# First batch: the halves of the squared norms enter through TensorE's accumulation

## The chip, the cores and the metric

One Trainium2 chip, one core of it. The metric is the time of one execution on the device in microseconds (us), the median of a few runs. Lower is better.

## The reference, cut to what matters

The reference is a linear attention with exponential random features, followed by two feed-forward layers over its output. The change is in the features of q and k, for the first of four batches:

```python
# q, k, v: (4 batches, 8 heads, 576 tokens, 64); omega: (128, 64)
q_s, k_s = q * 64**-0.25, k * 64**-0.25
def phi(x):
    proj = x @ omega.T                       # 128 features
    sq = np.sum(x * x, axis=-1, keepdims=True) / 2
    h = proj - sq
    h = h - np.max(h, axis=-1, keepdims=True)
    return np.exp(h) / np.sqrt(128)
...
num / den                                    # q' (k'^T v), q' sum(k')
# then x = (tokens, 512): g = h * sigmoid(1.702 h), h = x @ w_in (512 x 2048); x = g @ w_out
# then x = (x @ w_a * x @ w_b) @ w_out2, inner width 1536
```

Subtracting sq shifts all 128 features of a token alike, so the maximum over h, subtracted next, shifts with it.

## The kernel before, in words

The 576 tokens of a head are split into 512 (per batch eight heads make four pairs of heads, hp 0 to 3, with eight tiles of 128 tokens a pair) and a rest of 64 that is collected over the heads. The batches run one after the other; batch 0 has a way of its own. Its q and k stay in f32: for each pair of heads (named k0_0 to k0_3 and q0_0 to q0_3; the rests are k0_r and q0_r) `features` makes four transposes on TensorE into one bank of PSUM (L718), an eviction to SBUF that scales by 32 (L665 on ScalarE, L664 on VectorE for the names in `EVX`), and eight projections, f32 matmuls of 64 x 128 by 64 x 128 (L729): two heads, j 0 and 1, lie in the lower and the upper 64 rows of the array. The trace records each f32 matmul as two passes.

Beside that, ScalarE squares the raw tile in place (L762) and VectorE sums the squares (L764). When the projections are done, VectorE takes the maximum over the features, two reductions of 512 elements (L812), then two small operations form the bias of the exponential, first maximum minus sum (mh), then its negative minus sum (nb, L818). ScalarE runs eight exponentials with that bias (L778). For k, f32 matmuls with v accumulate the sums over tokens (L873, rest L871). For q, the features are transposed (L897), evicted (L899), multiplied with these sums (L904), divided by the denominator on VectorE (L929 to L934), and transposed (L959) into xT, the f16 high and low parts that the first feed-forward layer reads (L960, L961). The rests run through `rest_phase`, which has the same steps at half or quarter size (L673 to L706).

The weights arrive as raw words and are converted in chunks: four passes of 1024 elements per chunk on VectorE (L492, L532, L540, L499) and one on ScalarE (L550), for 16 chunks of the first layer and more later. The first layer's products (L992 to L994, L1027 to L1029) are dense f16 matmuls that begin when batch 0 is through; features of batches 1 to 3 (f16, L745, L746) are mixed in between. `fillers` issues matmuls whose result nobody reads (L1465, 15 in two calls of 5 and 10; ten more at the start, L1516).

The program is written out by generators that are stepped in turns, but the order on each engine's queue is not theirs: `ORDER` holds, for TensorE, ScalarE, VectorE and SyncE, one permutation of all instructions, and the last lines of the kernel tie each instruction to the one before it. An engine works through its queue strictly in that order. SyncE (SP) issues nearly all loads, so a load that waits for a buffer holds up those behind it.

Of the kernel before, what the change touches and what calls it, by code (L numbers as in the profile page):

```python
# [10 lines left out]
F32 = mybir.dt.float32  # L11
# [3 lines left out]
ALU = mybir.AluOpType  # L15
# [30 lines left out]
    "vKUb9t6x70/dp2+U5L228gZIhie6e74HO2/4pD23G/u9vd6DXQ62m7qz4HafDrb3cf90gyvDvxH3KW9g5o2X9O/BjZcs37tb3POR"
    "9yzkPQt5r/i6h6ke3tH9l+Puue6e6+657p7r7rnCvz/+8fHlvjT/zgiG9uXu4L7Vuu+ywl/v/ryje3Tr4Z+Suz//sHi/N4Dr7qDs"
    "wBG/95x8+nL/+vKa75/GSfFv3X3NN67y5a93V+MfxfuDlx/c77187+7+nsZyGu8ZrKd/zu5xdgZv2KYAudGUN5pSNN3rLe/1lm8P"
    "tqv7Su/rK6/v7UDc77kg7oVYDk750/338B7TdrbeHuKf7fuC7oPbcbmnp+7pKf/67k/vc9wH942IvhHR94i3nfqX976tvm+r7w7a"
    "v97+Od5/j+8/4vet9tOD7w+efnCf11u4128dv0OI8Xtw7qVR9+qpe/XUcULv4+5VUTfG68Z4+bXkBnrdQK8brHWDtcMvEPfJb+T0"  # L50
    "jZy+sdE3Njo85D55+uKdC5X7J7/P3ACusoP7tjyv30Ru/FV5H/cHNzb65YA5ko7L/ZNfQ9qh89O7KwfW7zU3/vqe5H770319NxL7"
    "nvO+J7SdmbdfZvw2c3+dubsaR+hGYt1IrPHX+9JuEJZfj+5dpe5dpe7rq/v66gZm3cCsG5h1A7ME5svjXnfPeb/c35HuYZ972Ofe"
    "Geb46T04NzrrLTbuTm901n0LJTpdTPfVz32DcwNunIp7kvv46/11rD3EL3N3zzeQ5gbN3PCZe5jmHqa5oTI3VOaGytwjPi97ubu/"
    "b2vu25qXv/rl7h7EG0h9/ODu4L7Bvu+t73vr4yH3EB8/uIf4hlSn3zjv425I9Q2pviHVQio97r6Pt98o76u6l8HcuH/eAOnyxbVw"
    "d3XjpW+8tHgpF87d1T15z3tInvdFPu/l93RZ+eUzffHr5f3BfS3P+1qe9xp8Pvzp/mJ6Y+15j+nzvt/nfftPb/9GxPO+86d3fmOj"
    "b2z0+Kkn8oP7ju7x63v8+uUhgvo+7u6g7eDlcfflvjzlfVXHq7rPcQ/O8x6c5z04z3sMnuUF3b/eUHn6nfketecNlefbr8x+x747"
    "uK/ldXfwsgO/n4uNe82Mg9O+56f31+z7HK/wO/z9bfu+wdd9g6/7Bl/3yV/3BLzuCXjd+Jt76OYeurnHeR52f0/ePQsjMI9f3u9m"
    "94le+0R3p2WnPj3cV3rP+as85O7q3lrm3lom/PXu+d5a5t435obF3BM694TOPaFzT+ikTzR3i3v8xtt3IMaf7u59SLl31pfPGmLD"
    "+3WF3mP1uqH8cpn6xOMjj888PvTc4zL70ec+m5frU9N9jhmfoe4W9znm6Xq7B6x9ue/cJXkP9txjOiXu707vcRkfysoZvOfoPtHT"
    "CbiX1eteVq/jOezqHr97Jb/al/tTH5k85X3NLxfx0w7uX4+36rXcx92bwuveFF4+ZfmY5bOZD183dl83bN/3Fvm+p/vlee/+xs3t"  # L60
    "huPccJwbjuMivuE4NxznhuO4c719rrxb3Pvu8+Favcfeh7n75XkP+/Me9ud9q8/jqrgPvjH5DJ8O7+PuXep5A+QZXtr9WOj6vaHy"
    "vKHyvKHyDKf7HqH7vK/7vO/7vO+Hz6j3A+IN0bfjci/J98MXn15ddPfZyqfR+2z3zDydmRuxzxuxT3epeySf7RPu3aJdW3eLe6af"
    "7Ynuu3SJ3wB53gB5+rwrCH3i9ZHXZ+T9kHyf456K59M94m7xcgNwH7pv+jg9zvl9q/csvO5ZeN2z8Lpn4XXPwuuehdfbgbhv8B7n"
    "9/Gq/PW+33uc3/c4v+9xfpdP0ven912+72F/O9gOrF2Fu8Dd/f3BK3zvBuF9yMuxT3ep+z7eNvN5/r7Ie+Jf95y/7sl7iat7Bl/O"
    "zD0Lr3sWXg9Xo1fls//96b3sX4kD7rb3sn/dy/6Vfnpf831V73tm3vcEvNsO7g/ug9/7kPvT+/re90J83x287w7e95bxvneBdzkQ"
    "952Pze5fkzzc11K+eCLPcX96z/77nv33PfvvwRB3p/f28L63h/c9++979t/3nL9vCLxvCLzFHzjBITcY3k97vju4V/f7Xt3ve0d6"
    "3zvS+17d7/H67Ap43Mf5BP6gAw888OADj1otwSV44cEXHoDhUbsVKnHEbti9b9i9b9i9X17lfaZ7V3i7K7iGbti9b9i9b9i9b9i9"
    "KQyG4TDC7u0JCMzj4QUt36zfLLastuCWR6zaeKEPLzT2q0eilsdZ1LFPNvFwgD/g44fw4sFtHuDmEWtF+9UuUceDmDzA0AMKPfjQ"
    "Aws9CNFjYejsk3sWvvMAPI/nfrWH5wKVP+f+2d7ozgP+PKjOg+g84M6DjzxQyQOTPDjJA5Q8XitSHo92Hr2PtC0peRCRxzoZJFsJ"
# [1549 lines left out]
```

## Time and profile before

| what | value |
|---|---|
| median of 3 runs | 864.57 us (863.15 to 868.79) |
| profiled execution | 867.92 us, span 866.1 us |
| TensorE (PE) busy | 854.5 us, 99% |
| VectorE (DVE) busy | 677.8 us, 78% |
| ScalarE (ACT) busy | 457.6 us, 53% |
| granted TensorE clock, mean | 0.999 |

The span is from the first to the last instruction of the profiled execution; the time beside it is that execution's own. "Busy" is the share of the span in which an instruction ran. Matmuls are pipelined and their ends are modelled, so the start of one matmul and the start of the next tell more of the pace than a duration does. PEld is the weight load, which runs beside the matmuls.

### The profile page before, as it was taken

How to read it: one execution, taken by the hardware profiler on the slowest of the kernel's cores; microseconds unless marked ns; L12 is line 12 of the kernel's file. 1: busy time of each engine (PE TensorE's matmuls, PEld its weight loads, DVE VectorE, ACT ScalarE, POOL GpSimd, SP SyncE). 2: the span in 40 equal slices, each digit the busy share in tenths (PEclk: the TensorE clock that was granted, in tenths of full speed). 3: DMA queues.
4: the chain of work that ended last, by engine and by line, in shares of the span. 5: the costliest groups of instructions: out<-in, count | busy, mean ns of one | idle time of the engine just before them, and what ended most of it. 6: DMA issues, size and time to landing. Idle time of an engine off the chain costs nothing.

```text
span 866.1 us, 17321 instructions
## 1 busy us (share of the span) xinstructions
PE 854.5 (99%) x7064; PEld 618.5 (71%) x7064; DVE 677.8 (78%) x1224; ACT 457.6 (53%) x1087; POOL 1.5 (0%) x11
## 2 busy tenths in 40 slices
PE   9999999999999999999999999999999999999997
PEld 7865555455554555444468888889888899888896
DVE  4999999999989987799111489968999658456766
ACT  5988786698668766654233554444543313123221
POOL 0000000000000000000000000000000000000000
PEclk9999999999999999999999999999999999999999
DMA  9766799866745344865110125322422203123312
GB/s 272 209 180 172 180 238 234 213 135 146 198 96 134 77 104 81 149 202 211 50 49 2 57 103 183 138 65 86 164 105 86 42 8 100 76 103 122 86 44 73
DMA packets 138735, 107.71 MB, mean 124 GB/s; under 512 B 107168, under 2 KB 120480, under 8 KB 136608
## 3 DMA queue, kind: packets, MB, share of 16 engines
q1 hardware_dynamic: 138080, 106.05, 44.9%
q8 instruction: 55, 0.90, 0.4%
q10 hardware_dynamic: 576, 0.56, 0.2%
q14 instruction: 24, 0.20, 0.1%
HBM read 71.07 MB, written 17.69 MB: 102 GB/s over the span
## 4 chain that ended last, share of the span: by engine, by line
PE 86%; DVE 8%; DMA 3%; ACT 2%; issue 1%; ACTq 0%; DVEq 0%
PE y L1027 6%; PE y L1028 6%; PE y L1029 6%; PE ph L994 6%; PE ph L993 6%; PE ph L992 6%; PE paA L1151 3%; PE paA L1153 3%; PE paA L1152 3%; PE pbA L1151 3%; PE pbA L1153 3%; PE pbA L1152 3%; PE oA L1247 3%; PE oA L1249 3%; PE oA L1248 3%; PE pa L729 1%
## 5 line engine op out<-in xcount | busy, mean ns | idle before, releaser
L1028 PE MATMUL y<-gl,w_out 128*128 128x512 f16 (+1 forms) x320 | 113.4, 358 | 0.4 <-DVE gl L1014 0.4
L1029 PE MATMUL y<-gh,w_out 128*128 128x512 f16 (+1 forms) x320 | 113.4, 358 | 0.0
L1027 PE MATMUL y<-gh,w_out 128*128 128x512 f16 (+1 forms) x320 | 109.5, 358 | 0.3 <-ACT gh L1013 0.3
L1014 DVE SCALAR_TENSOR_TENSOR gl<-th,gh 128x512 f16<-128x512 f32 (+1 forms) x80 | 50.4, 635 | 65.8 <-ACT gh L1013 65.4
L993 PE MATMUL ph<-xT,w_in 128*128 128x512 f16 x256 | 96.8, 379 | 0.0
L992 PE MATMUL ph<-xT,w_in 128*128 128x512 f16 x256 | 96.0, 379 | 0.2
L994 PE MATMUL ph<-xT,w_in 128*128 128x512 f16 x256 | 96.0, 379 | 0.0
L1151 PE MATMUL pbA<-forms,w_b 128*128 128x256 f16 (+1 forms) x240 | 61.1, 262 | 0.0
L1152 PE MATMUL pbA<-forms,w_b 128*128 128x256 f16 (+1 forms) x240 | 61.1, 262 | 0.0
L1153 PE MATMUL pbA<-forms,w_b 128*128 128x256 f16 (+1 forms) x240 | 61.0, 262 | 0.0
L1152 PE MATMUL paA<-forms,w_a 128*128 128x256 f16 (+1 forms) x240 | 61.0, 262 | 0.0
L1153 PE MATMUL paA<-forms,w_a 128*128 128x256 f16 (+1 forms) x240 | 61.0, 262 | 0.0
L1151 PE MATMUL paA<-forms,w_a 128*128 128x256 f16 (+1 forms) x240 | 61.0, 262 | 0.0
L1247 PE MATMUL oA<-w_o,ab 128*128 128x256 f16 x216 | 58.9, 273 | 0.3 <-DVE o L1255 0.3
L1249 PE MATMUL oA<-w_o,ab 128*128 128x256 f16 x216 | 58.9, 273 | 0.0
L1248 PE MATMUL oA<-w_o,ab 128*128 128x256 f16 x216 | 58.9, 273 | 0.0
L1161 ACT COPY ka<-paA 128x512 f32<-128x512 f32 (+1 forms) x30 | 16.3, 544 | 77.6 <-PE paA L1153 77.6
L1013 ACT ACTIVATE gh<-th 128x512 f16<-128x512 f32 (+1 forms) x80 | 47.0, 589 | 16.9 <-DVE th L1004 6.6
L1029 PEld LDWEIGHTS <-w_out 128*128 128x128 f16 x320 | 31.3, 98 | 29.0 <-issue 0.9
L993 PEld LDWEIGHTS <-w_in 128*128 128x128 f16 x320 | 31.3, 98 | 28.6 <-issue 1.4
L1161 ACT COPY kb<-pbA 128x512 f32<-128x512 f32 (+1 forms) x30 | 16.3, 542 | 66.4 <-PE pbA L1153 63.9
L994 PEld LDWEIGHTS <-w_in 128*128 128x128 f16 x320 | 31.3, 98 | 28.0 <-DVE w_in L499 0.4
(232 smaller groups left out, 2391.2 us busy)
## 6 DMA issues: line engine op xcount, KB each, us to landing
wraw<-in_moe_w_out_dram SPq DMA_DIRECT2D x14, 1024.0 KB, 6.3
forms<-fd SPq DMA_DIRECT2D x8, 1792.0 KB, 7.5
wraw<-in_moe_w_in_dram SPq DMA_DIRECT2D x8, 1024.0 KB, 5.7
fd<-forms SPq DMA_DIRECT2D x4, 1792.0 KB
wraw<-in_moe_w_a_dram SPq DMA_DIRECT2D x6, 1024.0 KB, 6.0
wraw<-in_moe_w_b_dram SPq DMA_DIRECT2D x6, 1024.0 KB, 7.5
vt<-in_v_dram SPq DMA_DIRECT2D x16, 256.0 KB, 5.5
rawq<-in_q_dram SPq DMA_DIRECT2D x16, 256.0 KB, 4.6
```

Of the source, the lines that this page charges most:

```text
L992: nc.tensor.matmul(ph[:, :n], w[:, 0, c, fs], xh(c), start=(c == 0), stop=False)
L993: nc.tensor.matmul(ph[:, :n], w[:, 0, c, fs], xl(c), start=False, stop=False)
L994: nc.tensor.matmul(ph[:, :n], w[:, 1, c, fs], xh(c), start=False, stop=(c == KC - 1))
L1027: nc.tensor.matmul(o, w[:, 0, f % 4, cs], gh[f][:, :n], start=(f == 0), stop=False)
L1028: nc.tensor.matmul(o, w[:, 0, f % 4, cs], gl[f][:, :n], start=False, stop=False)
L1029: nc.tensor.matmul(o, w[:, 1, f % 4, cs], gh[f][:, :n], start=False, stop=(f == FC1 - 1))
L1151: nc.tensor.matmul(o[:, i], wh, xh, start=first, stop=False, skip_group_check=True)
L1152: nc.tensor.matmul(o[:, i], wh, xl, start=False, stop=False, skip_group_check=True)
L1153: own["pe"] = nc.tensor.matmul(o[:, i], wl, xh, start=False, stop=final, skip_group_check=True).ins
L1247: nc.tensor.matmul(bank[:, t], lh, wh, start=first, stop=False, skip_group_check=True)
L1248: nc.tensor.matmul(bank[:, t], lh, wl, start=False, stop=False, skip_group_check=True)
L1249: nc.tensor.matmul(bank[:, t], ll, wh, start=False, stop=final, skip_group_check=True)
```

## The change

The sums of squares of batch 0 are no longer made by VectorE. ScalarE squares the transposed tile, read from PSUM, into the raw tile's place, and a second projection with a constant matrix `negs` (every element -1/PROJ = -256, PROJ being the scale that the exponential undoes) adds the negative sum of squares to every feature of the token in the same accumulation. The maximum is then taken over the finished difference, and one small operation makes the bias of it. `EVX` puts six evictions on VectorE instead of two. The memset that made a zero tile for the ten first matmuls now makes `negs`, and those matmuls read it. Batches 1 to 3 keep their way.

`ORDER` is planned anew for all four engines. TensorE has 6952 instructions instead of 6880, VectorE 1208 instead of 1224, ScalarE 1013 instead of 1017, SyncE 225 as before. Decoded, the first batch's part of it reads as follows. On TensorE the 72 projections of before stand in 14 unbroken blocks; 27 times two neighbours lie in opposite halves of the array, and 18 stand alone. The 144 of after stand in 9 blocks, 53 such neighbours and 38 alone, among these the last eight of k0_3 and all sixteen of q0_2. Fillers: before, 12 between the projections of k0_1 and the transposes of k0_3 and three before the sums of k0_1; after, five ahead of the fourth transpose of k0_0, one behind the transposes of k0_1, four between the transposes of k0_2 and k0_3, five ahead of the projections of q0_3. After the last projections of k0_3 come the transposes of q0_2, q0_1 and q0_3, then the projections of q0_r and q0_0, then the transposes of q0_r's features (L705), the sums of k0_3, and the projections of q0_1 and q0_2. On ScalarE the eight exponentials of k0_3 are followed by the eviction and the square of q0_1 and then q0_r's exponentials. On VectorE three steps of other work stand ahead of k0_3's second maximum, and three more ahead of q0_r's maxima.

```diff
 ORDER = (
-    "eNp93b2OK1mzINZXaVy7De74IylPgMYfQICcwRiCrHEkZyBH0Lur9gqyuvu7d2R09TlVzCSZGZmnuCJ2xP/zb//5P/3b//THf3n8"
...
 )
...
@@ -385,7 +387,7 @@
     CW, RB, FB = 256, 2, 2
     RW = CW // P
     START_W, LAG, POST_W, AL, EARLY = 0, 2, 8, 2, 3
-    VT, FILL, EVX = 4, 10, ('q0_1', 'q0_r')
+    VT, FILL, EVX = 4, 10, ('k0_1', 'k0_2', 'k0_r', 'q0_0', 'q0_3', 'q0_r')
     RAW = {"k": 3, "q": 4}
     SQACC = "1"
     EVD = ()
@@ -674,22 +676,23 @@
                 pt[:, u * P : (u + 1) * P], x[:, 2 * u : 2 * u + 2, :].rearrange("p n d -> p (n d)"), own["ident"]
             )
         scaled(f"{kind}0_r", xt.rearrange("p u m -> p (u m)"), pt[:, 0 : 2 * P])
-        sq, mx, mh, nb = (
-            pool.tile([P, NHP], F32, tag=f"rest{t}", name=f"{t}_rest{kind}", bufs=1) for t in ("sq", "mx", "mh", "nb")
+        mx, nb = (
+            pool.tile([P, NHP], F32, tag=f"rest{t}", name=f"{t}_rest{kind}", bufs=1) for t in ("mx", "nb")
         )
-        nc.scalar.activation(out=x, in_=x, func=AF.Square, scale=SQROOT)
+        x2 = x.rearrange("p n d -> p (n d)")
+        nc.scalar.activation(out=x2, in_=pt[:, 0 : 2 * P], func=AF.Square, scale=SQROOT)
+        x2 = x2.rearrange("p (u m) -> p u m", m=P)
         yield
-        nc.vector.tensor_reduce(out=sq, in_=x, axis=AX.X, op=ALU.add)
         pvs = [psp()[:, 0 : 2 * M].rearrange("p (u m) -> p u m", m=M) for _ in range(2)]
         for u in range(2):
             for j in range(2):
                 c = slice(j * D, (j + 1) * D)
-                nc.tensor.matmul(pvs[j][:, u, :], xt[c, u, :], om_f[c], start=True, stop=True)
+                nc.tensor.matmul(pvs[j][:, u, :], xt[c, u, :], om_f[c], start=True, stop=False)
+                nc.tensor.matmul(pvs[j][:, u, :], x2[c, u, :], own["negs"][c], start=False, stop=True)
         yield
         for j in range(2):
             nc.vector.tensor_reduce(out=mx[:, j::2], in_=pvs[j], axis=AX.X, op=ALU.max)
-        for o, i0, scale in ((mh, mx, PROJ), (nb, mh, -1.0)):
-            nc.vector.scalar_tensor_tensor(out=o, in0=i0, scalar=scale, in1=sq, op0=ALU.mult, op1=ALU.subtract)
+        nc.vector.tensor_scalar(out=nb, in0=mx, scalar1=-PROJ, scalar2=None, op0=ALU.mult)
         e = pool.tile([P, NHP, M], F32, tag="e", name=f"e_rest{kind}", bufs=2)
         for hp in range(NHP):
             nc.scalar.activation(
@@ -720,13 +723,17 @@
                     own["ident"],
                 )
             own["xt", nm] = scaled(nm, xt.rearrange("p u m -> p (u m)"), pt)
+            x2 = x.rearrange("p t d -> p (t d)")
+            nc.scalar.activation(out=x2, in_=pt, func=AF.Square, scale=SQROOT)
+            x2 = x2.rearrange("p (u m) -> p u m", m=P)
 
             def project():
 
                 for u in range(NT):
                     for j in range(2):
                         c = slice(j * D, (j + 1) * D)
-                        nc.tensor.matmul(pvs[j][:, u, :], xt[c, u, :], om_f[c], start=True, stop=True)
+                        nc.tensor.matmul(pvs[j][:, u, :], xt[c, u, :], om_f[c], start=True, stop=False)
+                        nc.tensor.matmul(pvs[j][:, u, :], x2[c, u, :], own["negs"][c], start=False, stop=True)
 
         else:
             x16 = pool.tile([P, T, 2, D], F16, tag="A", name=f"x16_{nm}")
@@ -746,8 +753,8 @@
                     nc.tensor.matmul(pv[:, u, :], xt[:, i, :], om_l, start=False, stop=True)
 
         groups, pairs = (GROUPS_F, PAIRS_F) if nm[1] == "0" else (GROUPS, PAIRS)
-        sq = pool.tile([P, T], F32, tag="sq", name=f"sq_{nm}")
-        TB = x.shape[1]
+        if nm[1] != "0":
+            sq = pool.tile([P, T], F32, tag="sq", name=f"sq_{nm}")
 
         def squares(lo, hi):
             for t in range(lo, hi):
@@ -759,9 +766,11 @@
             yield
             squares(0, NT)
         else:
-            nc.scalar.activation(out=x, in_=x, func=AF.Square, scale=SQROOT)
-            yield
-            nc.vector.tensor_reduce(out=sq[:, 0:TB], in_=x, axis=AX.X, op=ALU.add)
+            if nm[1] != "0":
+                nc.scalar.activation(out=x, in_=x, func=AF.Square, scale=SQROOT)
+            yield
+            if nm[1] != "0":
+                nc.vector.tensor_reduce(out=sq, in_=x, axis=AX.X, op=ALU.add)
         extra()
         yield
         if nm[1] in SQACC:
@@ -813,8 +822,11 @@
                     out=mx[:, ms], in_=pv[:, : len(g), :], axis=AX.X, op=ALU.max
                 )
                 if gi - 1 == pair[-1]:
-
-                    for o, i0, scale in ((mh, mx, PROJ), (nb, mh, -1.0)):
+                    if nm[1] == "0":
+                        nc.vector.tensor_scalar(
+                            out=nb[:, : z - a], in0=mx[:, : z - a], scalar1=-PROJ, scalar2=None, op0=ALU.mult
+                        )
+                    for o, i0, scale in ((mh, mx, PROJ), (nb, mh, -1.0)) if nm[1] != "0" else ():
                         own["nb"] = nc.vector.scalar_tensor_tensor(
                             out=o[:, : z - a], in0=i0[:, : z - a], scalar=scale, in1=sq[:, a:z],
                             op0=ALU.mult, op1=ALU.subtract,
@@ -1510,10 +1522,11 @@
         nc.scalar.dma_start(out=own["om"], in_=omega)
         a_load(att, "k", 0, 0)
         a_load(att, "k", 0, 1, nc.scalar)
-        zero = att.tile([P, 2, P], F16, tag="zero", name="zero", bufs=1)
-        nc.vector.memset(zero, 0.0)
+        own["negs"] = att.tile([P, M], F32, tag="negs", name="negs", bufs=1)
+        nc.vector.memset(own["negs"], -1.0 / PROJ)
+        zero = own["negs"].bitcast(F16).rearrange("p (a b) -> p a b", a=2)
         for _ in range(10):
-            nc.tensor.matmul(idle[:, 0:256], zero[:, 0], zero.rearrange("p a b -> p (a b)"), start=True, stop=True)
+            nc.tensor.matmul(idle[:, 0:256], zero[:, 0], own["negs"].bitcast(F16), start=True, stop=True)
         warm = att.tile([P, 1], F32, tag="warm", name="warm", bufs=1)
         nc.vector.memset(warm, 0.0)
         nc.scalar.activation(out=warm, in_=warm, func=AF.Exp)
```

## Rows read from the trace of the kernel before

**Rows 1.** The chain of work that ended last, shares of the span by engine.

```profile
PE 86%; DVE 8%; DMA 3%; ACT 2%; issue 1%; ACTq 0%; DVEq 0%
```

**Rows 2.** Stretches: us, then busy us (count) of PE, PEld, DVE, ACT, POOL; clock, DMA, GB/s.

```profile
5.00:17.40 12.40, 12.12 (x64) 9.46 (x65) 5.51 (x13) 7.04 (x20) 0.00 (x0) 1.00 1.10 277
17.40:60.00 42.60, 40.25 (x356) 34.55 (x354) 38.89 (x88) 38.08 (x132) 0.00 (x0) 1.00 0.73 201
60.00:360.00 300.00, 297.23 (x2195) 159.18 (x2195) 276.88 (x585) 217.69 (x605) 0.00 (x0) 1.00 0.66 154
```

**Rows 3.** Timeline of TensorE, 48 to 59 us: start, us, instructions, idle before.

```profile
47.99 0.38 PE L959 MATMUL pa<-ident,xf_q 128*128 128x128 f32 x2
48.82 1.11 PE L904 MATMUL pa<-kv,eT_q 128*128 128x65 f32 x8 [0.46 <-ACT eT_q L899]
...
57.50 0.50 PE L959 MATMUL pa<-ident,xf_q 128*128 128x128 f32 x3
58.78 0.22 PE L745 MATMUL pa<-om_h,xt_k 128*128 128x128 f16 x1 [0.78 <-DVE xf_q L934]
```

**Rows 4.** Groups on VectorE, 5 to 62 us: count, busy us, mean ns, idle before.

```profile
L540 DVE SCALAR_TENSOR_TENSOR wf<-wraw,wf 128x1024 int32<-128x1024 int32 x4 | 4.9, 1219 | 0.0
...
L764 DVE TENSOR_REDUCE sq_q<-rawq 128x8 f32<-128x512 f32 x4 | 2.7, 683 | 0.0
...
L664 DVE TENSOR_SCALAR xt_q<-pa 128x512 f32<-128x512 f32 x1 | 0.7, 682 | 0.0
L818 DVE SCALAR_TENSOR_TENSOR nb_q<-mh_q,sq_q 128x8 f32<-128x8 f32 x4 | 0.7, 164 | 0.0
...
L664 DVE TENSOR_SCALAR xt_restq<-pa 128x256 f32<-128x256 f32 x1 | 0.4, 417 | 0.0
L682 DVE TENSOR_REDUCE sq_restk<-restk 128x4 f32<-128x256 f32 x1 | 0.4, 409 | 0.0
```

**Rows 5.** Groups on ScalarE, 5 to 62 us.

```profile
L778 ACT ACTIVATE e_q<-pa,nb_q 128x128 f32<-128x128 f32 x32 | 8.9, 394 | 0.0
...
L762 ACT ACTIVATE rawq<-rawq 128x512 f32<-128x512 f32 x4 | 2.6, 651 | 0.2
...
L665 ACT ACTIVATE xt_k<-pa 128x512 f32<-128x512 f32 x4 | 2.4, 604 | 2.7 <-PE pa L729 2.3 <-PE pa L718 0.4
```

**Rows 6.** Timeline of TensorE, blocks of projections (L729) and what follows them.

```profile
23.33 1.16 PE L729 MATMUL pa<-om_f,xt_k 64*128 64x128 f32 x8
24.42 0.66 PE L718 MATMUL pa<-ident,rawq 128*128 128x128 f32 x4
...
28.71 0.66 PE L718 MATMUL pa<-ident,rawq 128*128 128x128 f32 x4
29.29 1.16 PE L729 MATMUL pa<-om_f,xt_q 64*128 64x128 f32 x16
30.38 1.11 PE L873 MATMUL pa<-vt,e_k 128*128 128x65 f32 x8
...
36.55 0.71 PE L729 MATMUL pa<-om_f,xt_q 64*128 64x128 f32 x8
37.20 0.98 PE L897 MATMUL pa<-ident,e_q 128*128 128x128 f32 x7
```

**Rows 7.** Timeline of TensorE, the fillers (L1465) and what follows.

```profile
13.15 2.74 PE L1465 MATMUL idle<-om_h 128*128 128x256 f16 x12
15.69 1.06 PE L718 MATMUL pa<-ident,rawk 128*128 128x128 f32 x4
16.68 1.58 PE L729 MATMUL pa<-om_f,xt_k 64*128 64x128 f32 x16
...
22.06 0.50 PE L1465 MATMUL idle<-om_h 128*128 128x256 f16 x3
22.40 0.39 PE L871 MATMUL pa<-vm,e_restk 128*128 128x130 f32 x2
```

**Rows 8.** Waits of SP's queue, 0 to 62 us: us in total, times, longest.

```profile
SPq L625 <- DVE sq_q L764: 7.4, 3, 3.7
```

More of the change, by code (lines that the diff above doesn't have):

```diff
@@ new lines @@
+    "p37+v+6+P8/XP8/VP9u0k/NE98j3lPKew/Nnm+fPNs+fbZ4/27x+/tc/W/S9FD/POT+Pv37+PT/bvO7z/fzu/fPv+TnU+2efudfr"
+    "Xryfc3jfK/jz+PPnv5/33z/7Pe9z/Dz2use5x/jZ5/Xz+Ote3HtFX/dq38v6/tnifS/vve7ve43vxX/fAbhX+X1HIQzDfey+lLeB"
+    "uiP1uL9/3PF53CM87haPO0SP+zSPe4zH3f9x9whHuv+6F/SU57xHMcj3Qp97hc+9jOdex3Mv9LlX+bTtnNzdZKeGg95D3Rlw7vU9"
+    "9/qee13PvbDnXtlzL825c+CkmXT3Tadxf2fC3BcTD/+6E8qLubPlpH/dI6fZ5z/vGdw5ctrv7nbtP+/h76Q5d/ac8cDddzxwn3I8"
+    "YJJ74B7vDu258+fcQT13RM8dynPnyHm6G7ys++gd03MH9dxRPXdYz507506aY3Rf7h03iu3ubm8b332N8J1B522Tu++dQMdAG/Y7"
@@ new lines @@
+    "vnEvdtyLHfdih5vO3XYvdri97sWOO+ZxxzzumMfD7+4eD0dxn94Le+dc3PkWd57FnWPhLt7b+B7lzq24syTuLAm3rXs23eV3X7fu"
+    "HYC4gxJ3FOIOaNwpFXdKxZ1IUTa5R7mDHHeQ0y1/D5r3oOnOd9A74aIcxR73oHcso71x3E3uIMcdy7hjHm2T+xx3uGNsd/e9Yx53"
+    "aOOOedzxjfF2dDe+gxxjj7vxHd+4kzXuZI07WeNO1rijH0/vYHePO/BxBz7uwMfL29jd4w583PGNO7RxhzvuSMcd37hDG2/vdfd4"
+    "d5DjzpK4cyNe/vMe/u3HPcod+Lz3Qt57Ie+9kPdeyId3UW+h99E7oHkHNI9H7zvbHfi8A5934PNOnzz2uI/e4c47kfJ44737emv0"
+    "/nyvZN6rm/fC5r2m2d6M77Pd65f3+uW9sHkvYt6LmPci5r2IeS9i3quWT++y93dhzO8T+QNxZ056x/cWf2dO7hv/PcqdJWmW3ImU"
@@ new lines @@
+    "dyLlnUh5J1LeCZJ3WmT58+ElOLW7xx3pvCOdd7Tyjlbe0co7WnnHKO/FzpfX5kzvHk973Oe4A5ovf4j8Z98/N/dvzz218lftnlo5"
+    "tTuMeQeq7vDUHa0yWncY8w5j3SGre9nrjlvda1938Op49D5wHOA+cK9V3WtV91rVvVblj6k/Wndy5Z1ceSdXvj2R0/D38p7unVz1"
+    "cOR70OOP8D3enSB1nIvTuNvd94267xvlD6q/rvcSl7+d5QF/de+h9m/q/c870nVHuu5I171+da9f3etXd+Dr6Y/v3eMOQIUf/ljf"
+    "H/fs6559vf3hvvvesy9nf69p3etXrt+9uv3wR/x1f9z/vJepwx/1+1f9XqZ2me4bSt03lEofE+6R0wOG8R75zrW686Xu6Ned/NU+"
+    "T9zt7uSvO/mrbXef8l77vteqfYbxYnzyuDdE3VlXPoDcWVf3/qh7f9TY457unTR9J03fSdMu9tPV8MD94OXTzL3s7TPLvex9L3v7"
@@ L302 @@
[L302 to L306 removed]
+    "24e3D28f3j68fXj78Pbh7cPbh7cPbx/ePrx9ePvw9uHtw9uHtw9vH94+vH14+/D24e3D24e3D28f3j68fXj78Pbh7cPbh7cPbx/e"
@@ L307 @@
+    "h5HeqIcPj59M233Pjw157MrQjQzsB40/YYz3N46wtp+/tv/8aPvOim/owCz4Tbjdm2zfO56/lP8L+H+c3g1Yv0GCP8mt+96R3wxX"
+    "t5xx69+wgrcL7xDeGv5kAu/7wjcf+SP28dX+P1m57jxvE+6+jXHEl/LrT9Ti/Eei30jGbyqtW9y4/C2V9vk/zsrdu9ZIuXP/pMi6"
+    "Gd1zbv7n+Wca7jeB9u8ZuP2bgfv6zbv9jX1sZu3rG+IwiIZt6f38JtU+fxH+N1l2Yb5/xf5PQu77m2P7J0X2b2mz/R9N/t/l2P49"
+    "Wfa//r//H7miBh4="
 )
```

519 lines of the change are left out of this document (251 added, 268 removed).

## The prediction

> **What bounds the kernel now.** I read the chain of work that ended last first. It puts 86% of the span on TensorE and 8% on VectorE [rows 1]. The stretches say where the 8% can be: TensorE is busy 297.23 of 300.00 us from 60 to 360 us, but 40.25 of 42.60 us between 17.4 and 60 us, where VectorE is busy 38.89 us and ScalarE 38.08 us [rows 2]. The change lives in that stretch and the 12.4 us before it. So the question is which engine ends that stretch, and the reader should look for TensorE standing still in it.
>
> The order of TensorE's instructions shows that it seldom does. Ends of matmuls are modelled, so I go by starts. Two transposes (0.11 us each) start at 47.99 and the next group at 48.82 us: 0.61 us lost, of which the view calls 0.46 idle. Three start at 57.50, the next at 58.78 us: 0.95 lost, 0.78 called idle [rows 3]. So true losses are about 1.26 times the idle shown, and the 2.35 us of the stretch [rows 2] become an estimated 3.0 us. From 60 to 360 us there are another 2.8 us at most. VectorE and ScalarE are nearly full beside TensorE, but TensorE is the one that hardly waits. **Whatever is added to TensorE must find its room in 3.0 + 2.8 us.**
>
> **What leaves VectorE and ScalarE.** VectorE loses eight sums of squares at 0.68 us and two of the rest at 0.41 (6.3 us), and of 20 small operations at 0.16 us ten remain, in another form that I price alike (1.6 us). It gains evictions: four of 0.68 and two of 0.42 in place of one of each, +2.5 us [rows 4]. Net -5.4 us, all of it work that stands beside TensorE's. ScalarE loses three whole evictions and a half one, some 2.2 us at 0.60 each [rows 5]. Its squares stay the same in number and read PSUM instead of SBUF; the eviction, which reads PSUM already, takes 0.60 against the square's 0.65 us, so I price this at nothing (ends -0.05 and +0.05 each). The merged memset and the filler's other operand cost nothing: same sizes, same engine. These savings shorten the end only through waits of TensorE that they remove.
>
> **What enters TensorE.** A further 72 projections, each recorded as two f32 passes. The price stands in their blocks of before. A block of 16 records on both halves of the array takes 1.09 us from its start to the next (29.29 to 30.38); 8 records on one half alone also take 1.09 us (23.33 to 24.42); 8 records on both halves take 0.65 us (36.55 to 37.20) [rows 6]. So a projection costs 0.22 us, a neighbour on the other half rides along free, and a block has 0.21 us of its own, plus 0.14 us before it: four transposes in front take 0.58 us, not 4 x 0.11. That is 0.35 us a block.
>
> Read from the two orders: before, 27 pairs and 18 alone in 14 blocks; after, 53 pairs and 38 alone in 9 blocks. That is 91 - 45 = 46 more times 0.22 us: +10.1 us; five blocks fewer: -1.8 us. Fillers: 12 ran at 0.212 us, 1.2 GHz, and three at 0.113 us, 2.4 GHz [rows 7] (the granted clock column reads 1.00 before 17.4 us too, but the early fillers show the half rate). After, ten come early and five late: -0.2 us. **TensorE: +8.1 us.** I take the full-rate price, though many added projections run at the half rate: TensorE is busy 12.12 of 12.40 us before 17.4 us [rows 2], so what is put there pushes other work past the rise.
>
> **What it can absorb.** Of the 3.0 us I take 2.0, since the gaps at 48 and 58 us sit in the normalisation of the last heads, which the change leaves as it is. Of the 2.8 us after 60 us I take half, 1.4, as VectorE, 5.4 us lighter, is further ahead with the weights.
>
> **What waits newly.** (a) The square is now between a head's transposes and its second projections: 0.65 us. Other heads' matmuls stand ahead of it in the order; if they run out it is 0.65 us at the first head. I take 0. No row of before has VectorE and ScalarE reading one bank of PSUM together, as six tiles now could, with eviction and square on different engines; even in sequence they take no longer than now, when ScalarE does both (0.68 + 0.65 against 0.60 + 0.65 us), so I keep 0, with 0.08 a tile as the upper end.
>
> The Trainium skill ("PSUM — Partial Sum Buffer", PSUM bank collisions raise a hardware error) says that two engines must not use one bank in the same partitions at once and that the compiler back end keeps them apart. By that the six pairs would run one after the other, each about 0.6 us later than side by side, an estimate of +3.4 us if TensorE waited for every one: 873.8 us against the median.
>
> (b) Five fillers stand ahead of the first head's fourth transpose, 1.06 us; the next transposes need a load in any case; 0, at most 1.06. (c) The raw tiles come free after the second projections, not after VectorE's sums. Already now the loads of raw tiles stand 7.4 us in SP's queue behind those sums [rows 8], with weight loads queued behind them. TensorE uses those tiles many us later, so I take 0, ends 0 and about 2 us for one late weight chunk (a conversion step is 1.22 us [rows 4]). (d) The transposes of the remainder of q. After the last eight projections of head k0_3 TensorE has 12 transposes, 12 pairs and two blocks: 1.3 + 2.6 + 0.7 = 4.7 us. In that time the other two must do a maximum and the bias (0.85 us), eight exponentials (2.2), an eviction (0.60), a square (0.65) and four exponentials (1.6) [rows 4, 5]: 5.9 us. So TensorE waits 1.2 us there. The path by VectorE has three more steps ahead of the remainder's maximum: 0.85 + 3 x 1.22 + 1.0 + 1.6 = 7.1 us, a wait of 2.4. I take 1.2. Queued behind it are head k0_3's own sums, two blocks of projections and all of the q phase.
>
> **Sum**: 8.1 - 2.0 - 1.4 + 1.2 = +5.9 us. The profiled execution took 867.92 us (span 866.1), so 873.8, or 0.68% more; against the median of the runs, 864.57 us, that is **870.4 us**.
>
> **Rivals.** 1, slower by more than 1%: the wait at the remainder's transposes is large. VectorE has three conversion steps ahead of k0_3's second maximum too; if they start late, up to 3.7 us come on top of the 2.4, and the old waits aren't recovered: 5.9 + 4.9 + 2.0 = +12.8, 877.4 us. It decides from a wait of about 4 us on. For it: VectorE is busy 91% of that stretch. Against: TensorE, being later itself, gives VectorE time to catch up. Chance 0.17.
>
> 2, no loss: the rate rises earlier. Now it rises inside the block that starts at 16.68 us, near 17.3, behind 12 dense fillers from 13.15 us, and not in the f32 work ahead of them [rows 7]. The new order has one long block of 32 projections right behind the first transposes, from 7 or 8 us by the prices above, 20 x 2 x 0.212 = 8.5 us long at half rate. If the rate rose in the middle of it, at about 11.6 us, 5.7 us at half rate would shrink by 2.9. With all 5.8 us of waits absorbed and no new one: 8.1 - 5.8 - 2.9 = -0.6, 864 us. The Trainium skill ("TensorE: Matmul & The Clock Gate", Part 1: The HAM clock gate) says that sustained activity releases the throttle; that speaks for this rival, but the trace's f32 work did not release it. Chance 0.14.
>
> 3, faster: VectorE ends the stretch, and the 5.4 us come off: 862.5, or 859.2 us against the median. For it: VectorE's 91%. Against: TensorE, at 94%, has no room for 8.1 us more. Chance 0.05.
>
> **How the numbers follow.** The forecast, TensorE's added work partly absorbed, +2 to +8.6 us, has 0.64. One per cent, about what a measurement can tell from no change, is 8.6 us. Faster by that needs more than rival 3 gives: 0.02. Slower: rival 1 and the forecast's upper edge, 0.22. Within: 0.76. The range 865 to 877 us leaves out rival 3, half of rival 2 and the upper part of rival 1, together about 0.2.
>
> **What would show it.** Right: the projections of the pairs of heads have 256 records in place of 128, in blocks at the prices above; the first dense products of the first feed-forward layer start some 5 us later; from there both traces run parallel. VectorE's stretch has idle time, or more conversion steps done by the same point. Wrong: TensorE idle for over 4 us at the remainder's transposes (rival 1); fillers or projections at the full-rate price before 15 us (rival 2); or TensorE's dense part starting no later than now (rival 3). A replanned order that costs or gives more than 3 us after 100 us would be outside all of these.

## The result, and the profile after

The changed kernel took 874.25 us (median of 4 runs, 873.12 to 875.91), the kernel before beside it 863.97 us: a ratio of 1.0106, 95% interval 1.0078 to 1.0134. In a later set of runs (e10 below) it was 870.92 against 865.50 us, 1.0068 (1.0043 to 1.0093). So it is slower, by 5.4 us in one set and 10.3 in the other. The forecast, 5.9 us more (870.4 us), lies near the lower of the two; why the sets differ is a part of what follows. The profiled execution took 874.63 us (span 872.8).

In the chain of work that ended last, VectorE's share halved, to 4% from the 8% of [rows 1]:

```profile
PE 88%; DMA 4%; DVE 4%; ACT 3%; issue 1%; SPq 0%; ACTq 0%; DVEq 0%
```

The same stretches as in [rows 2], same columns:

```profile
5.00:17.40 12.40, 11.47 (x128) 9.90 (x127) 5.27 (x12) 6.76 (x19) 0.00 (x0) 1.00 1.12 273
17.40:60.00 42.60, 41.26 (x410) 38.61 (x410) 40.28 (x75) 37.84 (x131) 0.00 (x0) 1.00 0.85 229
60.00:360.00 300.00, 296.52 (x2209) 159.31 (x2209) 271.84 (x584) 215.18 (x600) 0.00 (x0) 1.00 0.68 150
...
```

TensorE has 128 instead of 64 records before 17.4 us and 410 instead of 356 up to 60 us, and is idle 1.34 instead of 2.35 us in that second stretch. Its waits from 5 to 60 us (us in total, times, longest):

```profile
PE pa L916 <- ACT eT_q L911: 1.0, 2, 0.7
PE pa L675 <- DMA restk<-in_k_dram: 0.9, 1, 0.9
PE pa L735 <- ACT e_k L787: 0.2, 1, 0.2
```

Not one is for a square or a second projection. At the remainder's transposes (L708), where rival 1 had its wait, TensorE's timeline goes on without a gap:

```profile
33.35 0.27 PE L735 MATMUL pa<-om_f,xt_q 64*128 64x128 f32 x1
33.47 0.38 PE L736 MATMUL pa<-negs,rawq 64*128 64x128 f32 x2
33.78 0.55 PE L708 MATMUL pa<-ident,e_restq 128*128 128x128 f32 x3
```

Where eviction and square of one PSUM tile are on two engines, the square begins when the eviction has ended. VectorE's row, then ScalarE's:

```profile
22.00 0.69 DVE L666 TENSOR_SCALAR xt_q<-pa 128x512 f32<-128x512 f32 x1 [0.19 <-PE pa L721]
```

```profile
22.73 0.60 ACT L727 ACTIVATE rawq<-pa 128x512 f32<-128x512 f32 x1 [0.42 <-DVE xt_q L666]
```

All six such tiles show this, 0.03 to 0.05 us behind the eviction's end. From PSUM a square of 512 elements takes 0.59 to 0.66 us here (0.65 from SBUF, [rows 5]).

TensorE reached its upper clock at 5.0 us in this execution, at 17.4 in the profiled one of before. That is the first entry of each profile's record of the granted clock; the clock column of the stretches shows 1.00 ahead of it too, but the pace there is the lower one [rows 7]. Here the clock rose inside the five fillers: they ran in 0.70 us, start to next start, and the transposes behind them at 0.11 us each:

```profile
4.71 0.86 PE L1477 MATMUL idle<-om_h 128*128 128x256 f16 x5
5.41 0.71 PE L721 MATMUL pa<-ident,rawk 128*128 128x128 f32 x5
```

So the two profiles don't show the price of the change side by side: the one of before lost some 3 us to a late rise (2.7 at its end, by e5 below). And at 376 us the changed kernel has a stretch that before lacks (TensorE's timeline):

```profile
376.84 0.38 PE L1006 MATMUL ph<-xT,w_in 128*128 128x512 f16 x1
378.56 1.02 PE L1039 MATMUL y<-gh,w_out 128*128 128x512 f16 x4 [1.34 <-ACT gh L1025]
380.13 0.38 PE L1040 MATMUL y<-gl,w_out 128*128 128x512 f16 x1 [0.55 <-DVE gl L1026]
380.35 0.47 PE L1041 MATMUL y<-gh,w_out 128*128 128x512 f16 x1
380.61 0.63 PE L1040 MATMUL y<-gl,w_out 128*128 128x512 f16 x1
381.04 0.63 PE L1041 MATMUL y<-gh,w_out 128*128 128x512 f16 x1
```

The starts of the last two stand 0.43 us apart, twice the 0.215 us of the rows of 378 us: the granted clock of 380.5 to 384 us is 0.51, the lower level of 1.2 GHz (columns as in [rows 2]):

```profile
380.50:384.00 3.50, 3.50 (x11) 1.24 (x9) 3.50 (x7) 1.48 (x2) 0.00 (x0) 0.51 0.67 257
384.00:390.00 6.00, 6.00 (x29) 2.72 (x28) 4.34 (x6) 2.01 (x4) 0.00 (x0) 1.00 0.01 3
```

ScalarE's timeline says why gh is late. The conversion of w_a, which stands ahead of the Silu in its new order, waits for a sum of VectorE:

```profile
376.30 1.06 ACT L552 ACTIVATE w_a<-sx 128x1024 f16<-128x1024 f32 x1 [2.21 <-DVE sx L528]
377.26 0.58 ACT L1021 ACTIVATE th<-ph 128x512 f32<-128x512 f32 x1
377.87 0.63 ACT L1025 ACTIVATE gh<-th 128x512 f16<-128x512 f32 x1
```

A ruler for all the kernels: the rest of the program is the same in each, so I counted TensorE's work back from the end, every matmul at its full-rate time (0.213 us for 512 columns, 0.107 for 256 or for an f32 pass of 128 rows, 0.053 for a pass of 64 rows), and looked up when a given amount was left. With 790 us left the first batch is nearly done; between 500 and 440 us lies the stretch at 376 us. Where the order of small and large matmuls differs, a mark can fall up to about 1 us apart for the same state of the work. All in us of each trace:

```
                              790     700     500     440   span   upper clock from
before                       61.6   155.0   349.8   410.4  866.1   17.4
before again (e5)            57.9   152.7   347.2   407.8  863.4    8.7
changed                      64.5   154.9   352.3   417.2  872.8    5.0
changed again (e10)          64.6   155.5   349.7   413.4  869.0    4.6
e1  new front, old rest      64.3   157.0   353.3   413.3  868.9    4.2
e11 new to 330, old rest     64.5   155.0   352.6   412.7  868.3    4.9
e3  one moved                65.2   155.6   351.6   415.2  870.9    6.9
e9  two moved                65.3   155.7   350.4   412.7  868.3    5.7
e4  change in old order      66.9   161.9   357.1   417.2  872.8    9.1
e7  no sums                  55.9   148.6   343.8   404.6  860.2    4.1
e8  no squares               59.9   151.4   346.3   407.1  863.1   17.1
```

### The profile page after: what moved, and what is told of

Same layout as the page of the kernel before. It is cut to its first block, busy times and chain, and to the rows that moved or that the text cites. A ratio compares the mean times of both kernels' runs of the same rounds, so it can differ in the third digit from the quotient of the medians.

```text
span 872.8 us, 17582 instructions
## 1 busy us (share of the span) xinstructions
PE 858.9 (98%) x7208; PEld 624.7 (72%) x7208; DVE 674.8 (77%) x1208; ACT 456.3 (52%) x1083; POOL 1.5 (0%) x11
## 4 chain that ended last, share of the span: by engine, by line
PE 88%; DMA 4%; DVE 4%; ACT 3%; issue 1%; SPq 0%; ACTq 0%; DVEq 0%
PE y L1041 6%; PE y L1040 6%; PE y L1039 6%; PE ph L1004 6%; PE ph L1006 6%; PE ph L1005 6%; PE oA L1259 3%; PE paA L1163 3%; PE paA L1165 3%; PE pbA L1163 3%; PE pbA L1165 3%; PE pbA L1164 3%; PE paA L1164 3%; PE oA L1261 3%; PE oA L1260 3%; DMA eqT_q<-e_q 2%
## 5 line engine op out<-in xcount | busy, mean ns | idle before, releaser
L1041 PE MATMUL y<-gh,w_out 128*128 128x512 f16 (+1 forms) x320 | 115.1, 360 | 0.0
L1039 PE MATMUL y<-gh,w_out 128*128 128x512 f16 (+1 forms) x320 | 111.8, 358 | 1.5 <-ACT gh L1025 1.3
L1041 PEld LDWEIGHTS <-w_out 128*128 128x128 f16 x320 | 31.4, 98 | 29.7 <-issue 1.7
L1039 PEld LDWEIGHTS <-w_out 128*128 128x128 f16 x320 | 31.4, 98 | 29.4 <-issue 1.9
L1040 PEld LDWEIGHTS <-w_out 128*128 128x128 f16 x320 | 31.5, 98 | 28.1 <-issue 1.0
L1006 PEld LDWEIGHTS <-w_in 128*128 128x128 f16 x320 | 31.4, 98 | 27.8 <-issue 0.3
```

What stands on the lines that cost most here:

```text
L1006: nc.tensor.matmul(ph[:, :n], w[:, 1, c, fs], xh(c), start=False, stop=(c == KC - 1))
L1039: nc.tensor.matmul(o, w[:, 0, f % 4, cs], gh[f][:, :n], start=(f == 0), stop=False)
L1040: nc.tensor.matmul(o, w[:, 0, f % 4, cs], gl[f][:, :n], start=False, stop=False)
L1041: nc.tensor.matmul(o, w[:, 1, f % 4, cs], gh[f][:, :n], start=False, stop=(f == FC1 - 1))
```

## The experiments

**e5, the kernel before once more.**

> The kernel before, profiled once more. Theory A (its profiled execution of 867.9 us differs from its median of 864 because TensorE reached its upper clock at 17.4 us instead of near 5): this one reaches it before 10 us and takes 862 to 865 us. Theory B (the late rise belongs to the kernel's first batch): it rises near 17 us again and the time is 867 to 868 us.

865.18 us, span 863.4. The upper clock came at 8.7 us, inside the f32 work. TensorE's timeline shows the same 12 fillers in 1.32 us, start to next start, that took 2.54 us in [rows 7]:

```profile
11.24 1.48 PE L1465 MATMUL idle<-om_h 128*128 128x256 f16 x12
12.56 0.60 PE L718 MATMUL pa<-ident,rawk 128*128 128x128 f32 x4
```

Theory A, with the time 0.2 us above its range. By the ruler a rise 8.6 us earlier brought this execution 3.7 us ahead with 790 us left, 0.43 us each; with 700 us left 2.3 of them remain, at the end 2.7. An estimate from that: with a rise at 4.6 us, as in e10, it would be another 1.8 us ahead, 56.1 us with 790 left (e7, with a rise at 4.1 us, stands at 55.9), and by the same shares 1.1 us ahead with 700 left and 1.3 from 500 left to the end. The moment differs between executions of one program, so it is no part of the change.

**e4, the change in the old order; e7, the relief without the change.** e4 against the changed kernel, in words:

```diff
-EVX: k0_1, k0_2, k0_r, q0_0, q0_3, q0_r   (evictions on VectorE)
+EVX: q0_1, q0_r                           (as before)
-the changed kernel's order on PE, ACT, DVE, SP
+the order of before; each second projection behind its first, each square behind its eviction
```

> The change in the program (second projections, squares from PSUM, no sums of squares) with the issue order of the kernel before on every engine: each second projection right behind its first, each square right behind its head's eviction, the evictions on the engines that they had before. Theory A: 52 second projections of 0.22 us are 11.4 us, of which up to 5.5 us of waits in the first 60 us can be absorbed; with no loss at 380 us, 870 to 873 us. Theory B (the replanned order is what keeps the first batch's cost down, the rest costs nothing): 877 us or more, since the old order has waits where the new one has none.

873.57 us, 1.0103 (1.0080 to 1.0126): just above theory A's range, without a fall of the clock, and not theory B. (The expectation counts 52 second projections; the program has 72, since TensorE has 6952 instructions instead of 6880.) In the first set the changed kernel, with its replanned order, was no faster than this (1.0106), in the later one by 3 us (1.0068). Between 60 and 110 us TensorE has these waits in e4, and e5, the kernel before, has the two below them (timelines of TensorE):

```profile
64.01 0.22 PE L751 MATMUL pa<-om_h,xt_k 128*128 128x128 f16 x1 [0.78 <-DVE xf_q L945]
77.89 0.38 PE L1038 MATMUL y<-gh,w_out 128*128 128x512 f16 x1 [1.06 <-ACT gh L1024]
92.76 0.22 PE L751 MATMUL pa<-om_h,xt_k 128*128 128x128 f16 x1 [0.55 <-DVE kvl L847]
107.22 0.22 PE L751 MATMUL pa<-om_h,xt_k 128*128 128x128 f16 x1 [0.80 <-ACT e_k L786]
```

```profile
83.20 0.22 PE L745 MATMUL pa<-om_h,xt_k 128*128 128x128 f16 x1 [0.90 <-DVE kvl L836]
98.23 0.22 PE L745 MATMUL pa<-om_h,xt_k 128*128 128x128 f16 x1 [1.38 <-ACT e_k L778]
```

e7 is the kernel before, its order too, with this edit in the first batch:

```diff
-            nc.scalar.activation(out=x, in_=x, func=AF.Square, scale=SQROOT)
-            nc.vector.tensor_reduce(out=sq[:, 0:TB], in_=x, axis=AX.X, op=ALU.add)
...
-                    for o, i0, scale in ((mh, mx, PROJ), (nb, mh, -1.0)):
+                    nc.vector.tensor_scalar(out=nb, in0=mx, scalar1=-PROJ, scalar2=None, op0=ALU.mult)
```

> The kernel before in its own order, the first batch without its squares and its sums of squares (they fall out of h - max h). It is the relief that the change was to give VectorE, with nothing added to TensorE. Theory A (the sums held TensorE up for at most the 4 to 5 us of waits on VectorE in the first 60 us): 860 to 862 us. Theory B (the waits go over to ScalarE and the loads): 863 to 864 us, no change.

863.90 us, 0.9985 (0.9963 to 1.0008): no difference that can be measured, theory B. The two kernels share order and evictions; e4 has the second projections (and squares) more. Their ratios differ by 0.0118, 10.2 us, with an uncertainty of 2.8 from the two intervals: in the old order the second projections cost about their own time (11.4 us by the expectation's count), and all of VectorE's relief is worth 1.3 us at most likely (3.2 at the most, by the interval).

**e6, the changed kernel's order without the second projections.**

```diff
-nc.tensor.matmul(pvs[j][:, u, :], xt[c, u, :], om_f[c], start=True, stop=False)
-nc.tensor.matmul(pvs[j][:, u, :], x2[c, u, :], own["negs"][c], start=False, stop=True)
+nc.tensor.matmul(pvs[j][:, u, :], xt[c, u, :], om_f[c], start=True, stop=True)
...
-nc.scalar.activation(out=x2, in_=pt, func=AF.Square, scale=SQROOT)
```

> The changed kernel in its own order without the 52 second projections and the squares that feed them (the term they subtract falls out of h - max h, since it is the same for every feature of a row, so the negated maximum of the projections alone stands in for it). Theory A (the second projections cost their own time on TensorE): 46 times of 0.22 us go, 10 us, and with the waits of the later order left in place 864 to 866 us. Theory B (the waits of the first batch take their place, and the later order is what costs): 870 us or more.

875.20 us, 1.0102 (1.0066 to 1.0137): theory B by its time, and not as I had thought. Nothing came off, though 10 us of work did: counted by the ruler, e6 has 790 us left 0.7 us later than e10. TensorE ran dry in this order; its longest waits up to 70 us:

```profile
PE pa L906 <- ACT eT_q L901: 1.8, 2, 1.0
PE pa L961 <- DVE xf_q L936: 1.7, 1, 1.7
PE pa L685 <- DVE xt_restq L664: 1.5, 1, 1.5
```

and twice, at 26.3 and 46.8 us, near the end of the third and of the second of these, its clock fell to the lower level for 6.8 us (stretches, columns as in [rows 2]):

```profile
26.30:33.10 6.80, 6.38 (x38) 5.56 (x39) 6.44 (x13) 5.70 (x17) 0.00 (x0) 0.50 0.73 246
...
46.80:53.60 6.80, 6.47 (x31) 6.27 (x31) 5.35 (x13) 3.98 (x16) 0.00 (x0) 0.50 1.30 285
```

13.6 us at half rate are at most 6.8 us lost, the waits are the rest. How far the clock falls differs between executions: the mean granted clock of the seven runs is 0.982 to 0.996, and the slowest (878.35 us) has the lowest. Which of the new order's choices the waits come from is not shown: of these three, one is for an eviction by VectorE, and q0_r's is there in the old order too. So e6 gives no price for the second projections in the new order; that its pieces have none apart from the whole plan is argued, not shown.

**e1 and e2, the two halves of the new order.** Each engine's order is cut at a time of the trace; in e1 the changed program has its own order to 80 us, in e2 the program of before has its own to 66 us:

```diff
 e1, changed program:     own order to 80 us
-                         own order from 80 us on
+                         from 80 us on the order of before
 e2, program of before:   own order to 66 us
-                         own order from 66 us on
+                         from 66 us on the order of the changed kernel
```

> The changed program; its own issue order on every engine up to 80 us, the order of the kernel before for all that comes later. Theory A (part of the 10 us is lost in the replanned order of the later stages, at 371 to 384 us): about 870 us, 4 us below the changed kernel, and TensorE's granted clock does not fall at 380 us. Theory B (all of the 10 us comes from the first batch, as the prediction had it): 874 us, as the changed kernel.

> The program of the kernel before, its own order up to 66 us and the changed kernel's order for all that comes later. Theory A (the later order costs 4 us by itself): about 868 us, 4 us above the kernel before, with waits and a lower clock near 365 to 375 us. Theory B (the later order costs nothing): 864 us, as the kernel before. If the slip at 380 us needs the first batch's 3 us of delay as well, it is also 864 us.

e1: 871.26 us, 1.0093 (1.0064 to 1.0121), in its trace no wait and no lower clock near 380 us, as theory A had it. Its median is 3 us below the changed kernel's first one, but the two come from different sets: by the ratios (1.0093 and 1.0106) it is 1.1 us, and the intervals overlap, so no gain in time is shown. e2: 877.84 us, 1.0155, fits neither. It has a wait that neither kernel has and that the cut must have made:

```profile
PE ph L993 <- DVE th L1005: 10.7, 1, 10.7
```

with the clock at its lower level from 65.6 to 75.9 us. As a test by its time it failed. By the ruler, from 780 us left (79.6 us) to its end it takes 793.4 us, before 793.9: behind the cut the new order costs the old program nothing on the whole, though the other engines could run ahead in the long wait.

**e3 and e9, one and two instructions moved.**

```diff
 ScalarE: ye x4, w_a<-wf x2,
-  w_a<-sx, th, gh, w_a<-wf
+  th, gh, w_a<-sx, w_a<-wf
 VectorE, in e9 alone: ... wf (L542),
-  w_a<-sx,w_a (L501), gl (L1026)
+  gl (L1026), w_a<-sx,w_a (L501)
```

> The changed kernel with one instruction of ScalarE moved: the conversion of 128x1024 at 376.3 us of its trace goes behind the next Silu and its conversion to f16. Theory A (this instruction makes TensorE wait 1.34 and 0.55 us and then run 3.4 us at half its clock): 870.5 us, 3 to 4 us below the changed kernel, and the granted clock stays at its upper level through 380 us. Theory B (such waits are made up later, or come again a few us on): 874 us.

> The changed kernel with two instructions moved: ScalarE's conversion as in e3, and VectorE's gl of the same Silu (it waited there behind the last sum of w_a) one place ahead of that sum. Theory A (the two waits at 376 to 382 us are what the later order costs): TensorE's 1.95 us wait for gl goes too, 870.5 to 871.5 us, as e1. Theory B (the waits only move on, to the work on the weights that now is late): 873 us, as e3.

e3: 873.16 us, 1.0102 (1.0080 to 1.0124). The wait for gh shrank to 0.29 us, the one for gl grew from 0.55 to 1.78 (timeline of TensorE):

```profile
377.02 1.02 PE L1039 MATMUL y<-gh,w_out 128*128 128x512 f16 x4 [0.29 <-ACT gh L1025]
379.83 0.38 PE L1040 MATMUL y<-gl,w_out 128*128 128x512 f16 x1 [1.78 <-DVE gl L1026]
```

VectorE was now the late one: gl stands behind a sum of w_a that waits for the moved conversion. Theory B's "come again a few us on". e9: 871.14 us, 1.0070 (1.0045 to 1.0094); the wait for gl is gone, one of 0.84 for gh stays:

```profile
376.39 1.02 PE L1039 MATMUL y<-gh,w_out 128*128 128x512 f16 x4 [0.84 <-ACT gh L1025]
377.32 0.38 PE L1040 MATMUL y<-gl,w_out 128*128 128x512 f16 x1
```

By the ruler it passes from 500 to 440 us left in 62.3 us, e10 beside it in 63.7, e1 in 60.0. Its time is that of theory A, but e10, with nothing moved, had the same, so the move is not shown to gain anything.

**e10 and e11, the changed kernel again, and with the old order from 330 us.**

```diff
 e11, changed program:    own order to 330 us
-                         own order from 330 us on
+                         from 330 us on the order of before
```

> The changed kernel once more, for a second profile and for the same set of runs as e9 and e11. 873 to 875 us. If the fall of TensorE's clock at 380 us follows from the two waits before it, it is there again; if it was chance, the waits are there without it and the time is 1.7 us lower.

> The changed program, its own order up to 330 us, the order of the kernel before for what comes later. Theory A (the later order loses its 3 us at 371 to 384 us alone): 870.5 to 871.5 us, as e1. Theory B (it is lost between 80 and 330 us, where its trace has waits of about 1 us at 155, 185 and 195 us): 874 us, as the changed kernel.

e10: 870.92 us, 1.0068 (1.0043 to 1.0093), below what was expected. Both waits are there to 0.01 us, behind a third of 0.56 us for ScalarE that the first profile lacks; the fall of the clock is not there: the starts behind them stand 0.21 us apart.

```profile
369.70 0.38 PE L1039 MATMUL y<-gh,w_out 128*128 128x512 f16 x1 [0.56 <-ACT ye L1053]
...
374.68 0.38 PE L1006 MATMUL ph<-xT,w_in 128*128 128x512 f16 x1
376.39 1.02 PE L1039 MATMUL y<-gh,w_out 128*128 128x512 f16 x4 [1.33 <-ACT gh L1025]
377.97 0.38 PE L1040 MATMUL y<-gl,w_out 128*128 128x512 f16 x1 [0.55 <-DVE gl L1026]
378.18 0.38 PE L1041 MATMUL y<-gh,w_out 128*128 128x512 f16 x1
378.40 0.38 PE L1040 MATMUL y<-gl,w_out 128*128 128x512 f16 x1
```

Between 60 and 360 us it has a single wait of TensorE, 0.2 us. The first profile of the changed kernel had these there, at 156, 186 and 196 us and one more for a DMA at 351 us (us in total, times, longest):

```profile
PE pa L932 <- DMA eqT_q<-e_q: 1.8, 2, 1.0
PE pa L872 <- ACT e_k L787: 0.8, 1, 0.8
PE pa L752 <- ACT e_k L787: 0.7, 1, 0.7
```

By the ruler those are the 2.6 us between the two with 500 us left. By 440 another 1.2 come on top: the lower clock costs 1.7 us (3.4 us at half rate), e10's third wait makes up for some of it. So the later losses of the first profile were in part its own. e11: 870.08 us, 1.0052 (1.0031 to 1.0074), the lowest of the changed kernels, and 60.1 us from 500 to 440 us left (e10 63.7). Its median is 0.8 us below e10's, less than the intervals can tell apart, so by time it decides between neither theory. Its trace has the waits at 157 to 196 us and none near 376.

**e8, no squares at all.** The edit of e7 in every batch: 98 instructions fewer on ScalarE, 84 on VectorE.

```diff
-                nc.scalar.activation(
-                    out=x[:, t], in_=x[:, t], func=AF.Square, scale=SQROOT, accum_out=sq[:, t : t + 1]
-                )
...
-                            out=o[:, : z - a], in0=i0[:, : z - a], scalar=scale, in1=sq[:, a:z],
+                        out=nb[:, : z - a], in0=mx[:, : z - a], scalar1=-PROJ, scalar2=None, op0=ALU.mult
```

> The kernel before in its own order without squares and sums of squares in every batch: 98 instructions fewer on ScalarE and 84 fewer on VectorE, nothing on TensorE. Theory A (TensorE is the bound, and after 100 us loses only about 1.2 us in 50): 859 to 862 us, nearly all of the gain in the first 100 us. Theory B (the other engines' work is covered everywhere): 864 us.

860.86 us against 865.14, 0.9960 (0.9941 to 0.9979): theory A by its time, 0.4% faster than the kernel before. In its profile the clock rose as late as in that of before (17.1 and 17.4 us), so the two can be compared: 1.7 us ahead with 790 us left, 3.6 with 700, 3.0 at the end. That profiled execution took 864.91 us, the longest of the twelve, which fits the price of a late rise. The subtraction that the change gives to TensorE needn't be made by anyone, since h has the same term as its maximum; but even then most of VectorE's and ScalarE's freed time was beside TensorE's work.

## Why the prediction was right, point by point

- **TensorE's added work, +8.1 us: right.** With 790 us left e10 stands at 64.6 us, before (at the same rise of the clock, the estimate above) at 56.1: +8.5 us. The projections alone were sized somewhat low: in e7 their 14 blocks take 12.9 us, in e10 the nine take 23.4 (waits left out, both at the upper clock), +10.5, where the prices give 10.1 less 5 x 0.21 for the blocks, 9.1. The first block took 5.09 us, not 20 x 0.22 + 0.21 = 4.6. e4 against e7 bears the price out to no better than 2.8 us.
- **The rate.** I took the rise at 17.3 us for a property of the order. It was one execution's: 8.7 us in another of the same program. Rival 2 (the rise comes early, so no loss) had its sign in the trace, projections at the full-rate price from 7.5 us on, and still the kernel was slower. Eight profiles with the changed program or its order have the rise at 4.2 to 9.1 us, five with the program of before at 4.1 to 17.4; whether the change makes it earlier as a rule stays open. The Trainium skill ("TensorE: Matmul & The Clock Gate", Part 1: The HAM clock gate) has sustained activity release the throttle. e5 agrees so far that its rise came in the middle of f32 work, against my reading of [rows 7]; why the same work took until 17.4 us in the other profile no run here shows.
- **What is absorbed, 3.4 us: near in size, wrong in place and reason.** The 8.5 us became 3.9 with 700 us left (155.5 against 152.7 - 1.1), 4.6 us less, and 3.8 with 500. Most came back after 60 us, where I had put the smaller part, and not because VectorE is lighter. In e4 VectorE has the same sums taken off and fewer evictions, but the old order, and nothing comes back: it is 9.0 us behind e5 with 790 us left and 9.4 at the end (the clock rose at 9.1 and 8.7 us), with waits of TensorE of 0.78, 1.06, 0.55 and 0.80 us between 64 and 107 us. e5 has waits of 0.90 and 1.38 us there; e10, in the new order, has 0.17. So it was the replanned order, with its evictions, that made the room.
- **New waits.** (a) None for a square or its PSUM tile. The six pairs do run one after the other, as the Trainium skill has it ("PSUM — Partial Sum Buffer", PSUM bank collisions raise a hardware error), but the 3.4 us that would follow if TensorE waited for each did not come. The price of nothing was right. (b) The five fillers cost nothing: behind them TensorE waited 0.93 us for a load. (c) SP's queue waits longer, 9.2 us for the second projections (7.4 for the sums, [rows 8]), and TensorE's only wait for a raw tile up to 60 us, that one for restk, ends at 7.15 us, ahead of every projection. (d) The wait of 1.2 us at the remainder's transposes did not come: wrong, and rival 1 with it. From the end of k0_3's projections (28.35 us) to these transposes TensorE took 5.4 us, not 4.7, and the others 5.7, not 5.9 (ScalarE's last exponential ends at 34.02 us). The transposes go head by head: the first starts at 33.78, as the third exponential has ended. VectorE, far from late, stood idle for 0.61 us at 28 us, waiting for TensorE.
- **The step that failed: the later order at nothing.** I left the replanned order after 100 us out, as worth under 3 us. On the whole it is near nothing, but as two terms, each about as large as that mark. From 790 to 500 us left e10 gains 3.9 us on e1 (285.1 against 289.0); the first profile of the same kernel, with its waits, gains only 1.2 there. At 369 to 378 us e10 gives 3.7 back (63.7 against 60.0 us from 500 to 440 left). The rows show 2.9 of these, by the starts, in its three waits, for ye, gh and gl; the rest lies in where the mark of 500 falls in the two orders. The loss belongs to the new order: all six traces that run it through this stretch (changed, e10, e3, e9, and e2 and e6 without second projections) have waits for gh or gl there, and none of the others has. The change's end in e10 is thus 3.8 us at 500 us left, + 3.1 (60.6 us from there to 440 in e5, 63.7 in e10) = +6.9 us. With the waits at 156 to 196 us and the lower clock at 380 us, as in the first profile, it is 3.8 us more.
- **Luck in the sum.** Term by term e10 has 8.5 - 4.7 + 0 + 3.1 = +6.9 us, the forecast 8.1 - 3.4 + 1.2 = +5.9. That the two are near is in part luck: the wait of 1.2 us that did not come stood in for some of the 3.1 of the later order, and the room came from that order and not from VectorE's relief.
- **Rival 3** falls by e7: with all the sums gone and nothing added, VectorE's relief gives 1.3 us in the old order, 3.2 at the most, not 5.4.

What stays open: why the waits at 156 to 196 us come in some executions (changed, e3, e11) and only in part or not at all in others (e9, e10), why the clock falls in one and not in another, and how much of the 3 us between the changed kernel's two medians is theirs. The sets of e1 to e4, of e5 to e8 and of e9 to e11 also ran on three different chips, and no run tells a chip's part from chance. The medians of e1, e9, e10 and e11 lie within 1.2 us of each other, and their ratios to the kernel before (1.0052 to 1.0093) have intervals that overlap, so no run shows that a part of the later order costs time in the median.

## What to carry to other kernels

In this kernel, work moved to the engine that hardly waits cost about its own price, and the relief elsewhere paid only through that engine's waits: add those up first, and ask whether the order lets the relief reach them (e4 got none back, e10 4.6 us). An order planned for given durations is easily spoilt: with work taken out of it (e6) it lost as much as the work was worth, sewn to another (e2) it made a wait of 10.7 us. And before work is moved between engines, look whether it must be done: a term that is the same in a value and in its maximum is no work for anyone.

## What the runs showed of the hardware that was not expected

- TensorE's upper clock came between 4.1 and 17.4 us in near-equal first batches, 17.4 and 8.7 us in two executions of one program; by the ruler of those two 0.43 us lost for each us later with 790 us left, 0.31 at the end.
- Waits of 1.33 and 0.55 us, 1.0 us of work between them, were followed by 3.4 us at the lower clock in one execution and by none in another of the same program; a wait of 1.78 us in e3 was followed by none. In e6 two falls of 6.8 us each came near the end of waits of 1.5 and 1.7 us, and with the waits took back all that the removed work should have given.
